# Delta-rule attention followed by an MLP: weight conversion and weight fetches redistributed over the engines, with a new order of all steps

## The chip, the cores and the metric

The kernel runs on one core of a Trainium2 chip. A core has a matrix engine (TensorE, "PE" in the profile; its weight loads are listed apart as "PEld"), a vector engine (VectorE, "DVE"), a scalar engine (ScalarE, "ACT"), a general engine (GpSimd, "POOL") and a sync engine (SyncE, "SP") that issues transfers. ACT and POOL issue transfers too. Each engine works through its own list of instructions in the order in which they were written. An instruction may wait for others on other engines; everything behind it on its own engine then waits as well. The metric is the time of the whole program on the device in microseconds (us).

## What is computed

```python
def _attn_ref(q, k, v, beta):            # 4 batches, 8 heads, 768 positions, 48 wide
    k_n = k / (norm(k) + 1e-06)
    state = zeros((B, H, D, D))
    for t in range(S):
        kt, vt, bt = k_n[:, :, t], v[:, :, t], beta[:, :, t, None]
        y[:, :, t] = einsum('bhd,bhde->bhe', q[:, :, t], state)
        v_old = einsum('bhde,bhd->bhe', state, kt)
        state = state + bt[..., None] * einsum('bhd,bhe->bhde', kt, vt - v_old)
    return y

def _moe_ref(x, g_ln, w_ch1, w_ch2):     # x: the heads side by side, 4 x 768 x 384
    xn = (x - mean) / sqrt(var + 1e-06) * g_ln
    return x + maximum(xn @ w_ch1, 0) @ w_ch2      # 384 -> 1536 -> 384
```

The two weight matrices arrive in 64-bit floating point; everything else, and the result, is 32-bit.

## The kernel before

**Stages.** The 768 positions are cut into twelve chunks (0 to 11) of 64, and the recurrence over the positions becomes, per chunk, products of small matrices with one triangular inverse. The names in the step list follow that. For chunk c, `G` is the product of the keys with themselves (`gram`), `P` that of keys and queries (`queries`), and `recur(c)` does the recurrence itself: `u` (the corrected values), `y` (the output), `s` (the state), then the layer norm of `y`, two transposes of it (L1199) and the copies into `xnt` (L1217), which is what the MLP of the chunk reads. `mlp(c)` multiplies `xnt` with the first matrix (L1424 for chunk 0), takes the maximum with 0 (L1432), and multiplies with the second (L1466 for chunk 0).

**The beginning.** For chunk 0 the inverse is made on PE by five rounds of doubling block sizes (`first_inverse`): in each round, for each of two groups of heads, a product E (L785), a masked copy on DVE (L790), a product Z (L803), transposes on DVE (L750) and three copies on ACT (L744). For later chunks the inverse is made row by row on DVE (`rows_inverse`, L925 and L932).

**The weights.** The 64-bit weights are read as pairs of 32-bit words and converted on the chip, in twelve pieces of 128 x 768 numbers (six of the first matrix, then six of the second). Piece i (counted from 0 in the code, so `i < 3` are the first three) is fetched by `fetch(i)` with two transfers of 384 KB each, and `convert(i)` turns it into 32-bit numbers by four steps: `hi`, the exponent trick on the high words (ACT, L599); a shift of the high words (DVE, L604); `lo`, the low words scaled by 2**-29 (ACT, L607); and the sum of both as integers (POOL, L617). The first three pieces are converted in a left and a right half of 384 columns each, the others whole. The fetched words lie in five buffers: the third, fourth and fifth piece in `words` 0 to 2, the first and second in the two halves of `h_all`. The sixth piece goes to the buffer of the third, the seventh to that of the fourth, the eighth to that of the fifth, so each of these fetches has to wait until the piece that lies there has been summed.

**The order.** All 3032 steps of the program are numbered in the order in which the code makes them (`Line.add`). The text `ORDER` (L156 on) lists the numbers in the order in which they are written out (`Line.emit`), and `in_this_order` keeps each engine to it. So each engine's sequence of instructions is fixed by this list: 954 steps on PE, 814 on DVE, 489 on ACT, 443 on POOL, 332 on SP. A letter `f` in the list stands for one idle matrix product. The numbers used below are: 224, 232, 212, 228, 220, 216 the `lo` steps of the first three pieces (first right, third right, first left, second right, third left, second left); 222 the `hi` step of the first piece's right half; 233 and 221 the sums of the third piece, right and left; 91 and 92 the fetches of the second piece; 235 and 234 those of the sixth, 355/356 of the seventh, 361/362 of the eighth; 246 and 244 `lo` and `hi` of the sixth; 307 and 305 the last two of four loads of the keys of chunk 2; 310 and 309 their transposes on PE (L635), 312 and 311 the copies of these on ACT (L640); 209 the scaling of the values of chunk 0 (POOL, L689); 653 and 655 two key loads that POOL issues; 329 and 331 `u` of chunk 0 (L1087), 333 and 334 its `y` (L1113), 353 its state (L1123); 313 and 325 the products G of chunks 2 and 3 (L850); 321/322 and 323/324 transposes of the keys of chunk 3 and their copies; 347 the first transpose of the layer norm (L1201) and 348 to 350 its copies (L1217); 567 and 569 the first two groups of the MLP (L1424).

Of the kernel before, what the change touches and what calls it, by code (L numbers as in the profile page):

```python
# [10 lines left out]
ALU = mybir.AluOpType  # L11
# [145 lines left out]
51-52 54 58 53 55 57 319 56 63 62 306 398 67 308 393 66 320 7 65 64 9 8 59 61 60 249 11 10 48 12 49 654 656 50 248 68 0 3 2 13  # L157
71-72 46 40 44-45 42-43 41 101-102 1 75 36 82-84 76-77 73-74 37 103 38 104 99 93 39 94 100 90 85-86 78 15 14 69 208 87 89 105-108
16-18 79-80 70 81 110 88 111 114-118 121 119 113 120 124 112 122 25 19-20 125 123 132 126 134 6 5 22 133 30 128 127 33 21 23 135
232 92 97 218 130-131 129 230 220 109 258 253 251 140 137 222 136 91 138 27 31 141 139 142 146 34 143 152 148 24 26 147 158 32 154  # L160
153 231 210 96 145 144 149-151 157 155-156 95 160 159 162 164 161 163 168 28-29 169-170 98 205 165 207 206 174 166 212 167 173 172
171 255 254 252 257 256 395 307 305 176 317 402 405 318 401 47 233 175 178 177 219 184 180 185-186 655 653 658 226 214 182-183 238
188 181 242 187 189 192 259 240 221 209 f 4 179 193 190 194 191 215 223 35 211 250 260-262 241 263 265 201 197 202 204 236 199 203
200 198 309 195 310 264 243 235 234 228 362 237 239 196 329-333 335 353 311 355 312 224 356 361 313-314 354 266-268 337 269-270
338 341 216 315 246 271-288 342-343 289-295 427 321-322 324 323 334 429 336 325-326 347 339-340 348-350 327 344 316 396 399 296
404 406 217 213 328 225 303 298 302 403 301 300 299 468 304 469 426 297 466-467 394 397 400 244 567 569 568 428 345-346 351 571
570 357 572 245 227 352 657 659 229 247 666 660 430 575 593 363 576 359 579-580 594 431 573 583 599 432 407 365 574 584 600 587
577-578 588 358 364 661 410 408 392 409 366 360 605 581 591 368 582 592 606 470 367 411 611 585-586 412 597 589-590 413 598 379
374 612 595-596 603 369 371 601 630 604 602 373 434 1068 668 465 471-474 476-482 414 483-485 667 415 370 372 670 1067 391 669 665
416 609 418 610 420 380 417 631-632 615-617 433 375 419 421-422 633-635 607 618 385 425 386 423-424 435-436 608 381 377 613  # L170
619-620 783 785 782 787 486-498 376 499-507 382 508-511 671-672 378 512 673 383 513 384 1080 916 786 789 788 779 784 918 614 437
440 442 445 441 387 438 443 439 636 621 637 662 638-639 514 444 446-447 450 389 663 674-675 515 388 516 390 1070 1072 677 517 448
790 451 518 449 452 519-539 622-623 457 640 453 641 624-626 1174 780 664 924 676 926 681 540 680 678-679 541 543 542 544 475 642
627 460 456 454 459 458 791 455 794 821-822 825 827 826 831-832 823 828 837 682 824 833 838 843 792 645-647 651 648-650 683-686
848 845 1082 781 1069 688 1071 1073 1084 846 1083 1074 847 1079 545 793 546 834 839 548 550 547 549 551 553 552 555 554 795
689-700 556 829 796 840 830 844 797 835 854 864 917 928 1173 927 925 930 929 923 931 1179 1181 849 922 463 701-705 800 802 798 855
805 706 806 799 1075 856-857 836 865 858 801 841 859 810 842 860 921 1180 643 1183 644 628 1184 629 1185 1365 1171 1178 1182
919-920 932 557 1086 852 862 850 464 851 861 853 866-868 811-812 871 817 1085 461-462 1542 1081 863 803 652 804 933 869 881 872
882 934 807 558 561 819 818 560 559 562 707-710 808-809 711 936 870 712-717 813 883-885 889 886 873-876 878-879 1544 877 887 1087
1554 880 814 816 815 566 564 563 820 565 935 937 972 896-901 890-894 938 973 1546 888 1556 1545 1555 1558 1541 1543 1091 1559  # L180
718-719 1186 978 939 941 720-725 1548 996 726-729 940 895 730 902 731-751 687 1076 979 943 1077 984 974-975 942 907-910 1088 1190
911-912 980 944 946-947 945 913 985 1089 951 981 948 990 976-977 986-987 991 982 1005-1007 983 988 1008-1010 989 994 992 1361 1368
1360 1370 1369 1078 1172 1372 1176 752 904 903 905 1090 997 906 756 753-755 1366 1177 952 949-950 953 955 969 954 1092 956 1093
1367 1371 757-758 1187 768 960 1175 1094 958 1373 1362 1095 957 1374 914-915 959 759 1011 964 999 1002 998 967 1000 968 1547 1003
1012 1022 993 1032 1023-1025 995 1015-1016 1033 1017 760 762 761 763 766 764 767 1188-1189 1549 1191 965-966 1013 1001 1004 1014
765 1018 1026-1027 1019 1034-1036 1020-1021 1192 1040-1041 1037 1042-1045 1375 1030 1557 970-971 1219 1223 1653 1655 1657 1659
1363 1652 1193 1196 769 1194 1842 1648 1654 1656 1658 1840 962 1096 963 1038-1039 1029 1238 1031 1028 1097-1098 1046 1099-1100
2030 1102 1234 1220-1221 773 772 1198 771 1058-1062 1239 1047-1048 1195 1201-1202 770 1197 1199-1200 1203-1204 1103 1560 1224 1376
774 776 775 1206 1049 1063 1050-1052 777 961 778 1227 1553 1377 1064 1207 1104 1053 1105 1205 1106-1110 1208 1111 1101 1112
1235-1236 1228-1229 1237 1230 1251 1231-1232 1252 1210 1233 1240-1241 1209 1253-1254 1378-1379 1246 1242 1247 1222 1243-1244 1270  # L190
1261 1055 1225 1262 1226 1380 1561 1245 2032 1054 1280 1248-1250 1258 1255-1256 1263-1264 1259 1257 1266-1267 1265 1113 1660 1114
1260 1271-1272 1268 1115-1116 1281-1282 1381 1647 1211 1650 1845 1056 1215 1364 1214 1847 1057 1839 1213 1846 1212 1646 1065 1848
1841 1838 1844 1066 2034 1275 1273 1117 1283 1118-1120 1274 1269 1284-1286 1382 1308 1276-1277 1309 1298-1299 1310 1383 1311 1292
1289-1291 1296 1287-1288 1312 1300 1313 1293 1295 1121-1123 1278 1124 1305 1301-1303 1325 1216 1304 1279 1306 1326 1315-1317
1217-1218 1294 1297 1307 1408 2035 1327 1318-1320 1328 1324 1322 2036 1323 1415 2042 1384 1125 1314 1333 1329-1330 1334-1338
1126-1132 1331 1340-1341 1409 1342-1345 1133-1135 1339 1419 2031 1332 1550 1410 1351 1423 1321 1412 1352 1413 1136-1138 1346 1411
1353-1355 1416 1356 1417 1385 1551 1562-1563 1418 2033 1427-1428 1139-1143 1414 1144-1145 1357 1146-1165 1429-1430 1424-1425 1420
1432-1433 1421 1387 1426 1439-1440 1661 1422 1431 1837 1552 1645 1849 1564 1166 1569 1851 1358 1568 1169-1170 1167-1168 1359
1436-1437 2043 1442 1347 1443-1445 1438 1386 1446-1448 1441 1449 1434 1450-1454 1461 1348 1456 1455 1435 1651 1850 1649 1349 2138
1457 1462-1465 1470 1350 1473 1489-1490 1458 1466 1479-1480 1467 1491 1481-1484 1492 1390 1662 1388-1389 1391 1468 1459 1674 1469  # L200
1663-1664 1676 1460 1485 1471 1476 1496 1486 1472 1497 1493-1494 1498 1506 1499 1567 1566 1477 1474 1487 1565 1475 1478 1504 1488
1668 1395 1392 1665 1667 1666 1669 1570 1670 1673 1671-1672 1396 1495 1397 1393 1399 1507 1514-1515 1500-1501 1508 1516 1675 1677
1517 1509-1510 1518 1503 1519 1511 1394 1398 1571-1572 1855 1852 1573-1574 1577 1512 1576 1513 2029 1578 1520 1579-1580 1502 1400
1403-1404 1402 1401 2044 1505 1678-1683 1686 1581-1582 1687 1583 1684 1532-1535 1521 1853 1856 1405-1406 1536 1522-1523 1843 1685
2037 1860 1407 1524 1704 1537 1705 1525-1526 1711 1706 1715 1708-1709 1723 1857 1859 1691 1688 1854 1689-1690 1584 1692 1585 1527
1586 1693 1538 1694 1587-1588 1866 1858 1861-1862 1707 1863 1695 1868 1710 1712-1713 2140-2141 2143 2145-2146 2133 1529 1719 1747
1716 1724 1717 1714 1720-1721 1589-1590 1757 1725-1726 1738-1739 2046-2047 2041 1865 1722 1718 1735 1732-1733 1727 1736 1740-1741
1734 1864 1742-1744 1728 1591-1594 1737 1595-1597 1745 1598 1729-1730 1599-1602 1748-1749 1758-1760 1750 1696 1698 1700 2144 2142
# [47 lines left out]
def kernel(  # L256
# [13 lines left out]
    nc = tc.nc  # L270
# [99 lines left out]
    add = line.add  # L370
# [185 lines left out]
    def tb_nat(i, kinds=(0, 1)):  # L556
# [1214 lines left out]
```

## Time and profile before

| | us |
|---|---|
| median of 3 runs | 513.96 |
| lowest and highest run | 513.07, 515.15 |
| the profiled execution | 513.69 |
| span of its trace | 512.0 |

The trace covers all but 1.69 us of the profiled execution. On one core the page's first part gives the busy time of each engine; the second cuts the span into 40 equal slices (12.8 us each), where a digit is the busy share in tenths and `PEclk` the granted clock of PE. The answers about single stretches give, for each engine, the busy time in us with the number of instructions, then the granted clock, the share of time in which the transfer engines were busy, and GB/s. The timeline gives start, length, engine, line, operation, output and input, shape and count, and in square brackets how long the engine had been idle before it and what ended that. An engine name with a q is its queue issuing a transfer.

### The profile page before, as it was taken

To read this page: it belongs to the slowest core of one execution; us is meant where nothing else is said; L and a number is where in the kernel's file an instruction comes from. 1 tells how busy PE (TensorE), PEld (TensorE's weight loads), DVE (VectorE), ACT (ScalarE), POOL (GpSimd) and SP (SyncE) were. 2 spreads that over 40 slices of the span, in tenths; PEclk is the share of its full clock that TensorE was granted. 3 is DMA by queue.
4 is the path that set the end of the run, shared out by engine and by line. 5 is a ranking of instruction groups with operands and counts; after the bars stand their busy time and mean duration, and the time that the engine had idled before them with its cause. 6 is when DMAs were issued, how large, how long until landed. Compare 5 with 4: busy or idle time off the path is not lost.

```text
span 512.0 us, 22780 instructions
## 1 busy us (share of the span) xinstructions
PE 481.8 (94%) x9968; PEld 446.6 (87%) x9968; DVE 357.4 (70%) x814; ACT 206.2 (40%) x462; POOL 282.3 (55%) x447
## 2 busy tenths in 40 slices
PE   4677799999999999999999999999999999999997
PEld 3566697768898899899988999999999999999996
DVE  4847658897988667999868898688788436253241
ACT  4577744633443144323334522524513425324130
POOL 8024385224874996784465574634462831654554
PEclk9777999999999999999999999999999999999999
DMA  9986787559456855364644563734424601212011
GB/s 128 257 188 124 211 150 179 123 148 159 82 92 127 204 103 81 85 120 113 136 96 70 105 132 102 130 86 103 88 39 98 140 8 46 52 46 50 2 32 31
DMA packets 181635, 54.56 MB, mean 107 GB/s; under 512 B 164888, under 2 KB 177312, under 8 KB 181536
## 3 DMA queue, kind: packets, MB, share of 16 engines
q1 hardware_dynamic: 168512, 40.10, 38.9%
q10 hardware_dynamic: 10816, 9.83, 6.5%
q0 software_dynamic: 2208, 3.17, 4.0%
q8 instruction: 78, 1.28, 1.1%
q14 instruction: 21, 0.17, 0.1%
HBM read 36.30 MB, written 16.78 MB: 104 GB/s over the span
## 4 chain that ended last, share of the span: by engine, by line
PE 83%; DVE 6%; DMA 3%; issue 3%; SPq 3%; ACT 2%; ACTq 0%; DVEq 0%
PE f L1541 29%; PE f L1325 21%; PE f L1444 6%; PE two L837 3%; PE f L1424 3%; SPq L409 3%; PE by L1051 2%; PE two L1051 2%; PE f L1466 2%; PE two L1106 2%; PE two L1123 2%; PE by L1113 2%; DMA kr<-in_k_dram 2%; PE f L803 1%; PE by L785 1%
## 5 line engine op out<-in xcount | busy, mean ns | idle before, releaser
L1528 POOL TENSOR_TENSOR h_all<-h_all 128x256 f32<-128x256 f32 x99 | 73.5, 755 | 20.4 <-DVE tmp L925 8.4
L1541 PE MATMUL f<-w_sb,h_all 128*128 128x192 f32 x396 | 79.2, 330 | 0.0
L1541 PE MATMUL f<-words,h_all 128*128 128x192 f32 x396 | 77.3, 330 | 0.0
L1348 DVE TENSOR_TENSOR h_all<-f,h_all 128x512 f32<-128x512 f32 x72 | 49.0, 686 | 28.5 <-PE f L1325 21.8
L1541 PEld LDWEIGHTS f<-w_sb,h_all 128*128 128x128 f32 x396 | 65.0, 190 | 1.5 <-issue 0.2
L1541 PEld LDWEIGHTS f<-words,h_all 128*128 128x128 f32 x396 | 64.8, 190 | 0.8
L1566 POOL TENSOR_TENSOR words<-h_all 128x128 f32<-128x128 f32 x66 | 30.0, 472 | 54.0 <-ACT h_all L1352 28.5
L1343 ACT COPY h_all<-f 128x512 f32<-128x512 f32 x45 | 26.2, 585 | 81.3 <-PE f L1325 52.3
L932 DVE TENSOR_TENSOR xb<-xb,tmp 128x31 f32<-128x31 f32 (+19 forms) x139 | 53.6, 386 | 3.5
L925 DVE TENSOR_TENSOR tmp<-xb,gb 128x31 f32<-128x31 f32 (+19 forms) x139 | 51.7, 372 | 4.1 <-POOL xb L912 0.3
L1352 ACT ACTIVATE h_all<-h_all 128x512 f32<-128x512 f32 x54 | 32.5, 626 | 32.5 <-DVE h_all L1348 32.4
L409 POOL DMA_DIRECT2D tb<-in_k_dram x64 | 41.9, 657 | 0.9 <-issue 0.7
L1325 PE MATMUL f<-xnt,w_sb 128*128 128x128 f32 x288 | 39.6, 278 | 0.1
L1325 PE MATMUL f<-x_new,w_sb 128*128 128x128 f32 x288 | 39.5, 277 | 0.0
L1325 PEld LDWEIGHTS f<-x_new,w_sb 128*128 128x128 f32 x288 | 36.4, 192 | 0.3
L1325 PEld LDWEIGHTS f<-xnt,w_sb 128*128 128x128 f32 x288 | 36.0, 192 | 0.6 <-DVE h_all L1348 0.2
L1444 PE MATMUL f<-xnt,w_sb 128*128 128x256 f32 x144 | 33.8, 385 | 0.0
L1559 DVE TENSOR_TENSOR o<-f,x 128x192 f32<-128x192 f32 x33 | 11.3, 348 | 28.4 <-PE f L1541 18.3
L1444 PEld LDWEIGHTS f<-xnt,w_sb 128*128 128x128 f32 x144 | 26.7, 190 | 3.8 <-DVE o L1475 0.4
L1541 PE MATMUL f<-w_sb,words 128*128 128x192 f32 x132 | 26.4, 330 | 0.3 <-DVE o L1559 0.3
L617 POOL TENSOR_TENSOR w_sb<-words 128x768 uint32<-128x768 uint32 (+1 forms) x11 | 14.9, 1365 | 16.4 <-ACT words L607 14.7
L1541 PEld LDWEIGHTS f<-w_sb,words 128*128 128x128 f32 x132 | 21.5, 190 | 0.9 <-DVE o L1559 0.6
(237 smaller groups left out, 976.1 us busy)
## 6 DMA issues: line engine op xcount, KB each, us to landing
words<-in_moe_w_ch_dram ACTq DMA_DIRECT2D x20, 384.0 KB, 4.9
gd<-gsb SPq DMA_DIRECT2D x11, 512.0 KB, 3.7
v<-in_v_dram SPq DMA_DIRECT2D x24, 192.0 KB, 4.1
kr<-in_k_dram SPq DMA_DIRECT2D x46, 96.0 KB, 3.5
out_dram<-o SPq DMA_DIRECT2D x46, 96.0 KB, 2.4
xld<-xlt SPq DMA_DIRECT2D x9, 384.0 KB, 2.3
xnt<-xld SPq DMA_DIRECT2D x36, 96.0 KB, 2.9
tb<-in_q_dram SPq DMA_DIRECT2D x40, 64.0 KB, 3.7
```

Of the source, the lines that this page charges most:

```text
L409: add(eng, cost, lambda: QUEUE[eng].dma_start(out=out_, in_=in_), r, w, bulk=n * ns / 16e3, np=n, **kw)
L925: lambda j=j, n=n, w=w, t=t: nc.vector.tensor_tensor(out=t, in0=xv[:, 0:n, j : j + 1].to_broadcast([128, n, w]), in1=gv[:, j : j + 1, j + ...
L932: "DVE", dve(n * w), lambda t=t, rest=rest: nc.vector.tensor_tensor(out=rest, in0=rest, in1=t, op=ALU.subtract),
L1051: nc.tensor.matmul(dst[half(e), hp, j], src[drows(hp), (e if n else key_half(c, hp, e)) * GP + j], s_all[drows(hp), e, j], start=(n == 0 o ...
L1325: nc.tensor.matmul(wide(p[:, f : f + 128]), w[:, f : f + 128], r, start=start and i == 0, stop=True, skip_group_check=True)
L1343: add("ACT", act(512), lambda: nc.scalar.copy(o, p), pk, ok)
L1348: add("DVE", dve(512), lambda: nc.vector.tensor_tensor(out=o, in0=x, in1=y, op=op), [*xk_, *yk], ok)
L1352: add("ACT", act(512), lambda: nc.scalar.activation(o, o, ACTF.Relu, scale=scale), [], ok)
L1444: nc.tensor.matmul(p[:, 0:TOK], w1_sb[:, t, f * 128 : (f + 1) * 128], xnt[:, t], start=(t == 0), stop=(t == KC - 1))
L1528: add(eng, cost, lambda: e.tensor_tensor(out=out_, in0=x, in1=y, op=op), r, w, port=2 if eng == "Pool" else 1, pr=-2)
L1541: lambda f=f, t=start and f == order[0]: nc.tensor.matmul(p[:, 0:D2], lhs(f), rhs[:, f], start=t, stop=(f == order[-1]), skip_group_check=True
L1566: lambda f=f + i: e.tensor_tensor(out=s3[f], in0=one(0, 0)[0](f), in1=one(1, 0)[0](f), op=ALU.subtract),
```

## The change

Three things are edited.

```diff
-    RUN = 128
+    RUN, LOWS = 128, 3
...
         for a in range(2):
             dma(
-                "ACT", dst[:, a], src[:, a].rearrange("p (b x) -> p b x", x=2 * RUN), 384, 54,
+                "SP" if 5 <= i < 8 else "ACT", dst[:, a], src[:, a].rearrange("p (b x) -> p b x", x=2 * RUN), 384, 54,
                 w=[("wd", BUF[i], a)], after=after, **kw,
             )
...
-        add("ACT", 0.17 + 1.15e-3 * n, lambda: nc.scalar.mul(lo, lo, 2.0**-29), wk, lk, **kw)
+        if i < LOWS:
+            add("Pool", 0.19 + 1.67e-3 * n, lambda: nc.gpsimd.tensor_scalar(out=lo, in0=lo, scalar1=2.0**-29, scalar2=None, op0=ALU.mult), wk, lk, **kw)
+        else:
+            add("ACT", 0.17 + 1.15e-3 * n, lambda: nc.scalar.mul(lo, lo, 2.0**-29), wk, lk, **kw)
```

The six `lo` steps of the first three pieces go to POOL, and six transfers of 384 KB are issued by SP instead of ACT. The numbers of the steps stay what they were. The whole text `ORDER` is replaced; nearly all of its lines differ, and of the 954 PE steps 780 stand at another place among PE's steps, by at most 19 places. It has one `f` before and after. Taken apart by engine, the part that matters for the first 60 us is this (numbers in the order of the lists; `...` where steps are left out):

```
PE    before  ... 192 f 190 194 201 197 309 195 310 329 331 333 353 313 427 321 322 334 325 347 426 567 569 351 ...
PE    after   ... f 192 190 194 197 201 195 310 329 331 309 333 334 313 321 322 353 347 325 427 426 569 567 351 ...
ACT   before  ... 235 234 228 362 335 311 355 312 224 356 361 314 354 341 216 315 246 324 323 429 336 326 348 349 350 ...
ACT   after   ... 226 312 311 335 246 314 315 341 336 244 323 324 354 348 349 350 326 327 344 ...
POOL  before  65 64 9 8 59 61 60 249 10 ... 47 233 655 653 658 221 209 250 264 243 239 217 213 225 ...
POOL  after   9 10 65 64 59 7 249 654 46 8 ... 47 42 43 656 224 232 212 49 228 233 220 209 653 655 221 50 250 264 225 243 239 216 248 658 213 229 217 ...
SP    before  ... 395 307 305 317 402 405 318 401 316 396 399 296 ...
SP    after   ... 318 395 235 397 307 305 401 234 317 402 405 361 396 394 362 400 399 355 406 316 356 296 ...
```

On ACT, 91 comes right behind 222 in the new list, and 92 some way ahead of it. In the old list ACT has the `lo` steps 232 and 220 and the fetch 91 ahead of or around 222.

More of the change, by code (lines that the diff above doesn't have):

```diff
@@ L161 @@
[L161 to L172, printed above, removed]
@@ L249 @@
[L249 to L251 removed]
+53 51 56 55 58 57 9-10 65 64 52 54 2 11-12 33 13 3 0 63 66 62 306 320 319 308 59 7 249 654 46 8 44 40-41 45 48 60-61 47 68 72 71
@@ L252 @@
+2941 2926 2956 2946 2949 2957-2958 2980 2897 2889 2898 2888 2950 2959 2951 2960 2970-2974 2981-2982 2975 2983-2985 2976 2987-2989
+2986 2964 2961-2962 2967 2963 2968 3005 2990 3006-3007 2977 2997 2965 2978 2966 2969 2979 2998 2991-2992 2999-3001 3008 3002
+3009-3010 3003 2995 3004 2994 3012-3017 2996 3011 2993 3018 3023-3028 3019-3020 3029 3021 3030 3022 3031
 """
```

175 lines of the change are left out of this document (92 added, 83 removed).

## The prediction

> **What bounds the kernel now.** I read the page first, then the busy time by stretches, the timeline of PE, and the chain of waits for the first 66 us.
>
> ```profile
> span 512.0 us, 22780 instructions
> PE 481.8 (94%) x9968; PEld 446.6 (87%) x9968; DVE 357.4 (70%) x814; ACT 206.2 (40%) x462; POOL 282.3 (55%) x447
> ```
> ```profile
> 13.00:26.00 13.00, 7.99 (x296) 7.07 (x292) 10.93 (x33) 7.77 (x19) 0.81 (x2) 0.76 1.01 259
> 26.00:39.00 13.00, 9.38 (x324) 8.15 (x324) 6.59 (x20) 9.30 (x26) 4.07 (x6) 0.76 0.84 185
> 39.00:52.00 13.00, 9.72 (x338) 8.18 (x339) 9.66 (x31) 9.53 (x21) 5.06 (x6) 0.82 0.60 122
> 52.00:65.00 13.00, 10.13 (x308) 8.87 (x300) 8.05 (x32) 10.62 (x23) 5.30 (x7) 1.00 0.71 209
> 65.00:78.00 13.00, 13.00 (x320) 12.51 (x319) 7.87 (x14) 5.52 (x19) 11.39 (x13) 1.00 0.81 149
> ...
> 200.00:300.00 100.00, 97.64 (x1968) 93.18 (x1967) 86.52 (x185) 38.06 (x80) 61.53 (x104) 1.00 0.49 101
> ```
>
> PE is busy 94% of the span. What it lacks lies in front: in the four stretches from 13 to 65 us it is busy 7.99, 9.38, 9.72 and 10.13 us of 13, from 65 on 13.00 of 13. Later the worst stretch, 200 to 300, lacks 2.36 us. So the time is the moment at which PE becomes dense plus a mass of products that the change doesn't touch. An earlier start of the MLP of chunk 0 is worth its full length, as long as nothing later runs dry; work saved on ACT or added on POOL is worth nothing by itself. The start is here:
>
> ```profile
> 18.07 0.69 PE L785 MATMUL by<-qt,gsb 64*64 64x64 f32 x32 [3.67 <-DVE qt L773]
> ...
> 20.18 1.99 PE L803 MATMUL f<-xt,gsb 64*64 64x64 f32 x64 [0.82 <-DVE gsb L790]
> ...
> 43.68 1.15 PE L803 MATMUL f<-xt,pt 64*64 64x64 f32 x64
> 44.90 0.66 PE L635 MATMUL f<-ident,kr 128*128 128x128 f32 x4
> ...
> 46.91 0.65 PE L635 MATMUL f<-ident,kr 128*128 128x128 f32 x4
> ...
> 60.53 1.58 PE L1424 MATMUL f<-xnt,w_sb 128*128 128x128 f32 x12
> ```
> ```profile
> 50.79 0.84 issue
> ...
> 56.75 1.10 issue
> ```
>
> The last products Z of the inverse begin at 43.68; the key transposes 309 and 310 at 44.90 and 46.91; the MLP (567 and 569) at 60.53. From 310 to the MLP it is 13.6 us, with 0.84 and 1.10 us of it waits that the profile explains by nothing ("issue").
>
> **Part one: the six `lo` steps.** Each is an ACT instruction of 0.57 us:
>
> ```profile
> L607 ACT ACTIVATE h_all<-h_all 128x384 uint32<-128x384 uint32 x4 | 2.3, 568 | 0.0
> ...
> L1528 POOL TENSOR_TENSOR h_all<-h_all 128x256 f32<-128x256 f32 x99 | 73.5, 755 | 20.4 <-DVE tmp L925 8.4
> ```
> ```profile
> 33.64 0.61 POOL L490 COPY pt<-u 128x512 f32<-128x512 f32 x1 [19.83 <-DVE x L477]
> 34.22 0.82 POOL L617 TENSOR_TENSOR w_sb<-words 128x384 uint32<-128x384 uint32 x1
> 35.00 1.94 POOL L409 DMA_DIRECT2D tb<-in_k_dram  x3
> ...
> 39.00 1.47 POOL L689 TENSOR_TENSOR v<-v,knat 128x768 f32<-128x768 f32 x1
> ...
> 46.41 0.44 POOL L912 COPY xb<-db_b 128x16 f32<-128x16 f32 x1 [1.35 <-DVE gb L915]
> ```
>
> ACT loses 6 x 0.57 = 3.4 us. On POOL no row shows this operation. A copy with one input takes 0.61 us for 512 columns, so 0.46 by proportion for 384; a float operation with two inputs takes 755 ns for 256, so 1.13 for 384; the integer sum of the same 384 columns takes 0.82. I take 0.82, as the shape and type are the same, and keep 0.46 to 1.13. Three of the six (224, 232, 212) come where POOL sits idle for 19.83 us, until 33.64, and cost nothing there; were that idle time gone, they would cost 2.5 us. One, 216, comes behind 264, with the sums that the MLP's first group needs at 57 us. The other two, 228 and 220, come ahead of 209 and 221, and this is a new chain, worked out next.
>
> **Part two: the fetches on SP, and what they hold up.** The fetch 235 goes out only when 221 has summed the third piece. Behind it on SP now stand 397, then 307 and 305, the keys of chunk 2, which 310 and 309 on PE read, and behind these on PE stand 329 and the rest of chunk 0. Before, SP asked for these keys at 32.64, 12 us ahead of their use:
>
> ```profile
> 26.10 0.56 ACT L599 ACTIVATE h_all<-h_all 128x384 f32<-128x384 f32 x1
> ```
> ```profile
> 32.64 2.07 SPq L409 DMA_DIRECT2D kr<-in_k_dram  x2
> ...
> 58.40 0.63 SPq L409 DMA_DIRECT2D v<-in_v_dram  x1
> ```
> ```profile
> kr<-in_k_dram SPq DMA_DIRECT2D x46, 96.0 KB, 3.5
> ```
> ```profile
> DMA to landing us min/median/max: 3.4/4.9/7.6
> ```
> ```profile
> DMA to landing us min/median/max: 8.5/8.5/8.5
> ```
>
> (The last two are the transfers of weight words into `words` and into `h_all`.) In order: 222 runs at 26.10 before; its words are asked for a little later and ACT is a little freer, so I leave it. It ends at 26.7; the fetch 91 behind it takes 0.5 (an issue of SP takes 0.63), 27.2; the words land 4.9 later (the median into `words`; bounds 3.4 and 8.5), 32.1. POOL waits for them with 228: 0.82; 233: 0.82; 220: 0.82; 209: 1.47; 653 and 655: 2/3 of 1.94 = 1.29; 221: 0.82; together 6.0, so 38.1. SP then issues 235, 397, 307, 305: 4 x 0.63 = 2.5, 40.6. The keys took 3.5 by themselves, but now follow 384 KB of weights in SP's queue; I take the 4.9 of those (bounds 3.5 and 7.6): 45.5. **310 can start at 45.5, against 46.91.** Were the keys no bound, it could start when Z of the last round has ended, 43.68 + 1.15 = 44.8, less what the rounds themselves gain. They can gain at the very start:
>
> ```profile
> 6.31 0.23 DVE L442 TENSOR_TENSOR u<-u 128x64 int32<-128x64 int32 x1 [3.13 <-POOL u L436]
> ```
>
> DVE waits 3.13 us for an index pattern that POOL makes late; the new list has it as POOL's second instruction. Only part of that reaches the end of the rounds, since the keys of chunk 0 land later than this; I take 1 us of the possible 0 to 3.1, so 43.8 for the floor.
>
> The rule of the Trainium skill that bears on this is in "DMA: Bandwidth & Descriptors", section "Queues, rings and completion order": an engine takes the queue rows that have work in turn, but what stands in one row in order. By it the pieces would hurt more in SP's row, in front of the keys, than in ACT's, beside them. The bound 7.6 would then be the nearer one, the start of 310 at 48.2, and the whole time about 513.3. No row here shows a small load behind a piece in one queue.
>
> **Part three: from 310 to the MLP.** What ACT carries in that time sets it, as its instructions follow back to back:
>
> ```profile
> 45.31 0.91 ACTq L409 DMA_DIRECT2D words<-in_moe_w_ch_dram  x2
> ...
> 49.82 0.48 ACT L1151 COPY x<-two 128x384 f32<-128x384 f32 x1 [1.72 <-PE two L1113]
> ...
> 50.20 0.59 ACT L640 COPY kt<-f 128x512 f32<-128x512 f32 x1
> ...
> 51.15 0.57 ACT L607 ACTIVATE h_all<-h_all 128x384 uint32<-128x384 uint32 x1
> 51.15 0.63 ACTq L409 DMA_DIRECT2D words<-in_moe_w_ch_dram  x1
> 53.64 0.58 ACT L858 COPY gsb<-f 128x512 f32<-128x512 f32 x1 [1.92 <-PE f L837]
> 54.12 0.81 ACT L1135 COPY s_all<-two 128x768 f32<-128x768 f32 x1
> 54.81 0.31 ACT L1163 ACTIVATE rstd<-mv,eps 128x1 f32<-128x1 f32 x1
> ...
> 55.92 0.93 ACT L607 ACTIVATE words<-words 128x768 uint32<-128x768 uint32 x1
> ...
> 60.01 0.89 ACT L1217 ACTIVATE xnt<-by,g_sb 128x128 f32<-128x128 f32 x3
> ```
>
> Before, three `lo` steps (228, 224, 216: 1.7 us) and six issues (the first two 0.91, the last 0.63) lay in this stretch, and the state, the second `y` and the transposes stood in another order. After: 310, 329, 331 and 309 on PE take 2.5 us (0.65 for each set of transposes, 0.6 for each half of `u`). From then on ACT has 311 0.59, 335 0.48, 246 0.93, two copies 314 and 315 at 0.58, 341 0.31, 336 0.48, 244 0.93, two copies 323 and 324 at 0.59, 354 0.81, 348 to 350 0.89: 7.75 us. Behind 354 PE still has two sets of transposes (427, 426: 1.3 us), ending about when the copies do plus 0.5. So the MLP starts 2.5 + 7.75 + 0.5 = 10.7 us after 310, if nothing stalls; with the two waits of before (1.9 us) 12.7. I take the middle, 11.7: 45.5 + 11.7 = 57.2, against 60.53.
>
> **The sum.** -3.3 us at the start of the MLP. The six transfers that left ACT cost SP 6 x 0.63 = 3.8 us; beyond the keys they lie ahead of 316 and 296, which wait for copies and for DVE anyway, so 0 (a microsecond each for those if not). POOL's extra steps may slow DVE while both run: 0.2 us, a guess between 0 and the 2.5 of part one. The rest of the program, where 780 of 954 products change places, I put at 0, with -2.4 (the gap between 200 and 300) and +3 as ends. So -3.1: from the profiled execution's 513.69 (span 512.0 plus 1.69) to **510.6**. The median shown is 0.27 higher, within the spread of the three runs.
>
> **The rivals.**
>
> *More is won.* The keys arrive in time (30.6 for the second piece, 3.5 for the keys put 310 at its floor, 43.8) and no wait of the "issue" kind falls into the stretch: the MLP at 54.5, 6.0 earlier, 507.7. For it speaks that both waits have no cause in the profile; against it that each took the better end of its range. A full clock would help further: the granted clock is 0.76 and 0.82 from 13 to 52, and 64 products took 1.99 us there against 1.15 later. Of 27 us of PE work in these stretches a clock of 1.00 would take off at most 0.24 x 17.4 + 0.18 x 9.7 = 5.9. The 3.67 us for which PE waits ahead of 18.07 stay for the most part, so I expect the same two slow stretches. The Trainium skill, "TensorE: Matmul & The Clock Gate", Part 1, has the clock fall to half after a window of some 3.4 us without enough work; fewer gaps could so pay twice.
>
> *Given back later.* The MLP starts 3 us earlier, but its followers don't: DVE, 86.5 us busy of the 100 from 200 on, makes the row inverses, and PE waits for it at one of the chunks. 2.5 of the 3.1 come back: 513.1. For it speaks that PE was already dry by 2.36 us there; against it that the first row inverse (264 on POOL) starts at about 39 us, soon after 221, instead of 46.41, so DVE's chain moves up as well.
>
> *Slower: the new chain through POOL and SP.* Mechanism and place: 228 waits for the second piece at POOL's head, 221 behind it, 235 and the keys behind that on SP, 310 on PE. At the upper ends, 8.5 for the piece and 7.6 for the keys, 310 starts at 45.5 + 3.6 + 2.7 = 51.8, the MLP at 63.5, 3.0 us later than before: 516.7, and more if POOL takes longer for a `lo` than any row says. It decides against the change from a start of 310 at 60.53 - 11.7 = 48.8 on, 3.3 us behind my estimate. For it speaks that 8.5 was measured into the very buffer; against it that four pieces were under way then, and fewer here.
>
> *The edit does less than it says*: ACT's issues ran beside its operations (the one at 51.15 while ACT computed), so taking them off frees less than their length. This is in the sum, which counts only operations.
>
> **How the numbers follow.** A change of 0.5% is about what a measurement of this kernel can tell from none; that is 511.4 and 516.5. Forecast (-3.1; its own range 508.8 to 512.2) 0.50, of which 0.08 stays within 0.5%; more won 0.12; given back 0.14, mostly within, 0.03 slower; the chain through SP 0.24, 0.03 of it within. Faster 0.42 + 0.12 = 0.54; same 0.08 + 0.11 + 0.03 = 0.22; slower 0.03 + 0.21 = 0.24. The range goes from 506.5, a little beyond "more won", to 517.5, a little beyond the slower case.
>
> **What would show it.** In the changed kernel's timeline: six POOL steps of 0.46 to 1.13 us on 128x384 words, three of them before the second piece lands; SP idle ahead of the first `words` transfer until POOL's sum 221; the wait of the key transposes named "DMA kr"; the MLP's first group at 57 (54.5 to 60); ACT without gaps ahead of it; from 65 on PE busy as before. I am wrong if the first group starts after 60.5, or if it starts near 57 and the stretches behind it lack as much PE time as the front gained.

## The result, and the profile after

| kernel | chip | median us | runs | ratio to the kernel before, 95% interval | mean granted clock of the runs |
|---|---|---|---|---|---|
| before | first | 512.95 | 18 | 1 | |
| changed | first | 509.76 | 18 | 0.9937 [0.9919, 0.9955] | 0.989 |
| before | fourth | 512.63 | 22 | 1 | 0.982 |
| changed, measured again | fourth | 510.97 | 12 | 0.9982 [0.9955, 1.0009] | 0.987 |

In the first measurement the changed kernel is faster by 0.6%. In the second, on another chip, it is faster by 0.2%, and that interval includes 1, so this measurement alone does not tell the change from none. The forecast was 510.6 us. The profiled execution of the first measurement took 510.69 us, 1.69 more than its span.

The page of the changed kernel, span and busy time:

```profile
span 509.0 us, 22783 instructions
...
PE 480.2 (94%) x9968; PEld 445.5 (88%) x9968; DVE 362.7 (71%) x814; ACT 204.5 (40%) x456; POOL 289.8 (57%) x453
```

The stretches of the changed kernel that were shown of the one before:

```profile
13.00:26.00 13.00, 8.55 (x284) 7.26 (x272) 9.11 (x29) 8.12 (x21) 4.39 (x5) 0.74 0.97 264
26.00:39.00 13.00, 9.98 (x324) 8.63 (x324) 7.17 (x24) 8.99 (x25) 8.62 (x10) 0.74 0.70 164
39.00:52.00 13.00, 9.46 (x405) 8.11 (x400) 12.10 (x37) 9.99 (x21) 7.88 (x9) 1.00 0.73 165
52.00:65.00 13.00, 11.73 (x242) 10.89 (x237) 7.72 (x22) 10.01 (x25) 6.98 (x9) 1.00 0.93 219
65.00:78.00 13.00, 12.16 (x377) 11.07 (x369) 8.25 (x22) 5.12 (x16) 6.29 (x9) 1.00 0.80 186
91.00:104.00 13.00, 11.18 (x279) 7.29 (x278) 11.80 (x19) 5.87 (x10) 10.67 (x12) 1.00 0.69 151
...
200.00:300.00 100.00, 98.73 (x1978) 94.46 (x1981) 87.16 (x186) 36.62 (x74) 63.00 (x104) 1.00 0.52 109
```

The stretch from 91 to 104 in the kernel before:

```profile
91.00:104.00 13.00, 13.00 (x356) 9.14 (x358) 10.57 (x24) 8.24 (x15) 4.89 (x4) 1.00 0.61 131
```

The reader is to see two things. From 52 to 65 PE is busy 11.73 us instead of 10.13: the MLP has begun earlier. And a new hole has opened from 91 to 104 (11.18 of 13, where it was 13.00), where DVE is busy 11.80 and POOL 10.67. From 65 to 78 PE is busy 12.16 instead of 13.00, so part of the gain is given back there already. The timeline of PE in the changed kernel says where:

```profile
16.16 0.69 PE L789 MATMUL two<-qt,gsb 64*64 64x64 f32 x32 [2.90 <-DVE qt L777]
...
43.62 0.66 PE L639 MATMUL f<-ident,kr 128*128 128x128 f32 x4 [0.44 <-ACT xt L748]
...
55.27 0.39 PE L1428 MATMUL f<-xnt,w_sb 128*128 128x128 f32 x2
56.35 1.38 PE L1428 MATMUL f<-xnt,w_sb 128*128 128x128 f32 x10 [0.70 <-POOL w_sb L621]
...
103.21 0.55 PE L1205 MATMUL by<-ident,xln 128*128 128x128 f32 x3 [1.82 <-DVE xln L1173]
```

The first E is 1.9 us earlier than before, the key transposes 310 are 3.3 us earlier (46.91 before), the MLP 5.3, or 4.2 if one counts from 56.35, where it runs on. In the trace of the second measurement (N below) these are 1.2, 2.4 and 3.5 us (E at 16.85, 310 at 44.54, the MLP at 57.06). At 103.21, ahead of the transposes of chunk 1's layer norm, PE waits 1.82 us for DVE. The chain on POOL and SP that the prediction worked out, in the changed kernel:

```profile
26.03 1.24 POOL L609 TENSOR_SCALAR h_all<-h_all 128x384 uint32<-128x384 uint32 x1
...
28.01 1.21 POOL L609 TENSOR_SCALAR h_all<-h_all 128x384 uint32<-128x384 uint32 x1 [0.46 <-DVE words L605]
29.29 0.83 POOL L621 TENSOR_TENSOR w_sb<-words 128x384 uint32<-128x384 uint32 x1
...
34.29 0.85 POOL L621 TENSOR_TENSOR w_sb<-words 128x384 uint32<-128x384 uint32 x1
```
```profile
35.30 1.68 SPq L410 DMA_DIRECT2D words<-in_moe_w_ch_dram  x1
...
37.65 1.31 SPq L410 DMA_DIRECT2D kr<-in_k_dram  x2
```

In one execution each of the kernels F, K and M below PE ran far slower (690.28, 958.45 and 689.52 us); these are left out of the ratios, and as the profiled execution of F and K was such a one, no times of PE are taken from those two traces.

### The profile page after: what moved, and what is told of

Same layout as the page of the kernel before. It is cut to its first block, busy times and chain, and to the rows that moved or that the text cites. A ratio compares the mean times of both kernels' runs of the same rounds, so it can differ in the third digit from the quotient of the medians.

```text
span 509.0 us, 22783 instructions
## 1 busy us (share of the span) xinstructions
PE 480.2 (94%) x9968; PEld 445.5 (88%) x9968; DVE 362.7 (71%) x814; ACT 204.5 (40%) x456; POOL 289.8 (57%) x453
## 3 DMA queue, kind: packets, MB, share of 16 engines
q8 instruction: 78, 1.28, 1.1%
## 4 chain that ended last, share of the span: by engine, by line
PE 80%; DVE 9%; issue 3%; DMA 2%; ACT 2%; SPq 2%; POOL 2%; DVEq 0%
PE f L1545 28%; PE f L1329 23%; PE f L1448 6%; DVE xb L936 3%; PE two L841 3%; PE by L1055 2%; PE f L1470 2%; PE two L1055 2%; PE by L1117 2%; PE two L1110 2%; SPq L410 2%; DVE tmp L929 2%; PE f L1428 2%; PE two L1127 1%; PE by L1009 1%
## 5 line engine op out<-in xcount | busy, mean ns | idle before, releaser
L936 DVE TENSOR_TENSOR xb<-xb,tmp 128x31 f32<-128x31 f32 (+19 forms) x139 | 59.8, 430 | 3.8
L1312 POOL TENSOR_TENSOR x_new<-xnt 128x128 f32<-128x128 f32 x27 | 13.0, 486 | 23.2 <-PE f L1329 10.6
```

Of the source, the lines that this page charges most:

```text
L936: "DVE", dve(n * w), lambda t=t, rest=rest: nc.vector.tensor_tensor(out=rest, in0=rest, in1=t, op=ALU.subtract),
```

## The experiments

Each kernel was compared with the kernel before on the same chip: A to D on one, F, G, H and J on a second, K, L, M and the changed kernel again (N) on a third, the "fourth" of the table above. The two columns in the middle are from one trace each, in us.

| kernel | first MLP product | first MLP product of chunk 1 | median us, all runs | ratio, 95% interval | mean granted clock of the runs |
|---|---|---|---|---|---|
| before | 60.53 | 112.91 | 513.40, 513.49, 512.63 | 1 | 0.982 on each of the three chips |
| changed | 55.27 | 110.01 | 509.76 | 0.9937 [0.9919, 0.9955] | 0.989 |
| changed again (N) | 57.06 | 110.61 | 510.97 | 0.9982 [0.9955, 1.0009] | 0.987 |
| A | 59.36 | 114.22 | 512.30 | 0.9980 [0.9953, 1.0007] | 0.984 |
| B | 54.70 | 108.53 | 510.49 | 0.9963 [0.9939, 0.9988] | 0.989 |
| C | 55.76 | 111.14 | 511.50 | 0.9971 [0.9951, 0.9991] | 0.987 |
| D | 61.31 | 113.47 | 513.25 | 1.0014 [0.9985, 1.0043] | 0.981 |
| F | | | 511.63 | 0.9954 [0.9926, 0.9982] | 0.988 |
| G | 57.40 | 111.06 | 510.57 | 0.9942 [0.9918, 0.9965] | 0.986 |
| H | 57.62 | 111.58 | 513.46 | 1.0003 [0.9972, 1.0035] | 0.983 |
| J | 58.87 | 110.50 | 510.66 | 0.9948 [0.9920, 0.9976] | 0.989 |
| K | | | 518.60 | 1.0102 [1.0061, 1.0143] | 0.979 |
| L | 55.57 | 107.77 | 508.43 | 0.9904 [0.9873, 0.9936] | 0.990 |
| M | 55.96 | 107.15 | 509.00 | 0.9914 [0.9882, 0.9947] | 0.989 |

Two rows of one and the same kernel (changed, N) lie 1.8 us apart at the first MLP product. N's inverse starts 0.7 us later, and its PE stands 1.28 us more, at 53.97, for what the profile calls "issue". So a single trace shows mechanisms well and sizes under 2 us badly. The clock adds to this: PE's granted clock falls to 0.50 for some us at a time, and not at the same places in each trace. It is 0.50 from 34 to 43 us in the kernel before and from 31 to 37 in the changed one, and even from 48 to 58 in A and from 51 to 57 in J, where it makes the first MLP product late.

### Which part of the change does it: A, B, C, D

A keeps the new order alone; B adds the fetches on SP to it, C the `lo` steps on POOL; D has both edits in the old order.

```diff
 A and B
-    RUN, LOWS = 128, 3
+    RUN, LOWS = 128, 0
 A and C
-                "SP" if 5 <= i < 8 else "ACT", dst[:, a], ...
+                "ACT", dst[:, a], ...
 D
 ORDER = """
-53 51 56 55 58 57 9-10 65 64 52 54 2 11-12 33 13 3 0 63 66 62 306 ...
+51-52 54 58 53 55 57 319 56 63 62 306 398 67 308 393 66 320 7 65 64 ...
```

> The new order, with all lo steps and all fetches on ACT again, at their places in the list. Theory 1 (the MLP of chunk 0 starts earlier because ACT is relieved between 43 and 57 us): ACT gets back three lo steps among the rounds and one (216) plus six issues around 310, and the two fetches of the eighth piece stand ahead of the key copies and wait for POOL's sum of the fifth piece (43.6 to 45 us in the changed kernel); first MLP product at 57 to 58 instead of 55.3, ratio to the kernel before 0.997 (0.995 to 1.000). Theory 2 (the order does it alone, the two moves are incidental): first product at 55 to 56, ratio 0.994.

> The new order and the three fetches on SP, but the six lo steps on ACT (0.57 us each instead of 1.24 on POOL). Theory 1: ACT has 1.7 us more among the rounds and 0.57 around 310, POOL's chain to the sum 221 has 2 to 3 us less; first MLP product at 56 to 57, ratio 0.995 to 0.998. If POOL's chain to 221, SP's fetch and the keys were the bound, this kernel would be faster than the changed one: first product before 55, ratio 0.992.

> The new order and the six lo steps on POOL, but all fetches on ACT. Theory 1: the eighth piece's fetches hold the key copies on ACT until the sum of the fifth piece, about 45 us; first MLP product 1 to 2 us later (56.5 to 57.5), ratio 0.996 to 0.998. If the queue of SP behind the fetches (keys, gram, row inverse) was what cost time, this kernel is faster: ratio 0.992 or less.

> The old order of all steps with both moves. Theory 1 by ACT's load alone: from u of chunk 0 to the MLP ACT carries 1.7 us of lo steps and six issues less, so the first MLP product at 58.5 to 59.5 instead of 60.5, ratio 0.996 to 0.998. Theory 2 (order alone): ratio 1.000; slower than before if the longer lo steps on POOL (1.24 us) hold up the row inverse of chunk 1 or the sums: 1.002.

A, fetches on ACT; the timeline of PE around 310, then that of ACT:

```profile
42.74 0.63 PE L639 MATMUL f<-ident,kr 128*128 128x128 f32 x4 [1.07 <-DMA words<-in_moe_w_ch_dram]
...
48.88 0.77 PE L1117 MATMUL by<-u,pt 64*64 64x48 f32 x17 [3.01 <-issue]
```
```profile
43.75 2.29 ACTq L410 DMA_DIRECT2D words<-in_moe_w_ch_dram  x2
...
46.98 1.05 ACT L644 COPY kt<-f 128x512 f32<-128x512 f32 x2
```

And B, fetches on SP, the timeline of ACT:

```profile
43.90 0.59 ACT L644 COPY kt<-f 128x512 f32<-128x512 f32 x1 [0.36 <-PE f L639]
```

The wait ahead of 310 is longer with the fetches on ACT (1.07 us in A and 1.61 in C, put down to a transfer of `words`, against 0.44 in B, put down to ACT), but 310 does not start later for it: at 42.74 and 43.70, against 43.24 in B and 43.62 in the changed kernel. What the fetches hold is ACT's next work. In A they go out at 43.75, when the first of two sums on POOL has ended, and the copies 312 and 311 of the transposed keys follow at 46.98 (47.06 in C); in B the first of them runs at 43.90. So the fetches did hold ACT's copies, by some 3 us, and moving them removes that. How much of it reaches the MLP is not shown: C has its first product at 55.76 all the same, and A's 59.36 contains the 3.01 us of "issue" and the stretch at half the clock. B reaches the first MLP product at 54.70 with all `lo` steps still on ACT: in this one trace the `lo` steps were not needed on POOL for an early start. None of the four came out in the range that its first theory gave for this product (57 to 58, 56 to 57, 56.5 to 57.5, 58.5 to 59.5). B's is the value that was to speak for POOL's chain as the bound, but its ratio is not the 0.992 that belonged to it. By time the four cannot be ranked: A, B and C lie between 0.996 and 0.998, and the full change, measured on two other chips at 0.9937 and 0.9982, lies on both sides of them. What stands apart is D: in the old order both edits together gain nothing, and its interval lies above that of the first measurement of the whole. D was expected at 0.996 to 0.998. Its trace, POOL and then PE:

```profile
59.65 2.39 POOL L623 TENSOR_TENSOR w_sb<-h_all 128x384 uint32<-128x384 uint32 x3 [5.39 <-DVE xb L938]
```
```profile
61.31 1.60 PE L1430 MATMUL f<-xnt,w_sb 128*128 128x128 f32 x12 [1.49 <-POOL w_sb L623]
```

In the old order the last three sums of the first pieces stand on POOL behind the row inverse of chunk 1 on DVE, and the MLP waits for them. The edits need an order made for them. Whether the order alone (A, whose interval just includes 1) gives less than the whole is not shown.

### What brought the beginning forward: G and K

G writes the two index patterns 9 and 10 behind five other POOL steps. K gives POOL's first 21 steps the order of before, but behind them three `lo` steps stand ahead of the copies 43 and 41, and 221 with its fetches 235 and 234, as well as 361 and 362, stands later. So K changes more than the copies.

```diff
 POOL, changed kernel and G
-9 10 65 64 59 7 249 654 46 8 ...
+65 64 59 7 249 9 10 654 46 8 ...
 POOL, changed kernel and K
-9 10 65 64 59 7 249 654 46 8 44 40 41 45 48 60 61 47 42 43 656 ...
+7 65 64 9 8 59 61 60 249 10 48 49 654 656 50 248 46 40 44 45 42 224 232 212 43 41 228 220 47 ...
```

> The changed kernel with the two index patterns as sixth and seventh instruction of POOL instead of first and second. Theory 1 (they are what brought the inverse of chunk 0 forward): the first E goes from 16.2 back to about 18 us, the key transposes 310 and the MLP come 1 to 2 us later, the ratio is 0.996 to 0.998. Rival (the keys of chunk 0 and ACT set the start): the first E stays at 16 to 16.7, the ratio stays at 0.993 to 0.995.

> The changed kernel with POOL's first 24 steps in the order of the kernel before: loads and a large fill first, the eight copies of 512 columns from about 10 us on. Theory 1 (these copies, standing beside DVE's chain of short steps for the first keys, stretch it; moved ahead of it they brought the first E forward): the short DVE steps between 9 and 14 us take 0.4 to 0.7 us instead of 0.15 to 0.2, the first E goes from 16.2 to 17.5 to 18.5, the MLP starts 1 to 2 us later, the ratio is 0.996 to 0.999. Rival (the order on DVE, ACT and PE did it): the first E stays below 16.8, the ratio stays at 0.993 to 0.995.

The first E of G, in the timeline of PE:

```profile
16.06 0.69 PE L792 MATMUL two<-qt,gsb 64*64 64x64 f32 x32 [2.75 <-DVE qt L780]
```

The theory of G falls: E stays at 16.06, and the ratio at 0.9942. In G DVE takes up the second pattern at 5.05 us (1.44 in the changed kernel, 6.31 in the kernel before), and still waits for the keys behind it. The wait of 3.13 us for a late index pattern, which the prediction credited with 1 us, was covered by the wait for the keys. In its place the timelines of the kernel before, DVE and then POOL, offer this:

```profile
9.86 0.61 DVE L665 TENSOR_TENSOR ndb<-knrm 128x8 f32<-128x8 f32 x1
...
13.25 0.57 DVE L665 TENSOR_TENSOR ndb<-knrm 128x8 f32<-128x8 f32 x1
```
```profile
9.85 0.61 POOL L490 COPY pt<-u 128x512 f32<-128x512 f32 x1
...
10.98 2.28 POOL L490 COPY xt<-u 128x512 f32<-128x512 f32 x4
```

The same step in the changed kernel, where POOL's copies have begun at 5.43 us, while DVE waits for keys:

```profile
9.02 0.17 DVE L669 TENSOR_TENSOR ndb<-knrm 128x8 f32<-128x8 f32 x1
```

0.57 and 0.61 us beside POOL's copies, 0.17 without them, for eight numbers a row. K was to show that these copies set the first E. The first half of its theory holds: beside the copies the step takes 0.57 and 0.45 us on DVE again. The rest cannot be read: K is 1.0% slower than the kernel before, far beyond what was expected of it, and the moved copies got a wait that had not been counted. K's timelines of POOL and DVE:

```profile
22.88 1.28 POOL L494 COPY xt<-u 128x512 f32<-128x512 f32 x2 [11.01 <-DVE xb L469]
```
```profile
29.83 0.42 DVE L797 COPY_PREDICATED gsb<-x,by 128x256 f32<-128x256 int32 x1 [6.15 <-POOL gsb L494]
```

POOL stands 11.01 us ahead of the copies; three `lo` steps follow, and only then the copy into `gsb` for which DVE, in the middle of the inverse, waits 6.15 us. So K shows that POOL's first steps can cost more than the whole change brings, and leaves open how much of the 1.9 us comes from the copies beside DVE. That reading stands on the rows of the kernels and was not shown by an experiment of its own. A rival was not tested: the second group of transposes of chunk 0's keys (PE, L635 and L639) starts at 9.91 in the kernel before and at 8.86 in the changed one, both times after a wait put down to the keys' transfer, so earlier keys may be a part of it.

### How much room the new chain has: H

```diff
-lambda: nc.gpsimd.tensor_scalar(out=lo, in0=lo, scalar1=2.0**-29, ...)
+lambda: [nc.gpsimd.tensor_scalar(out=lo, in0=lo, scalar1=x, ...)
+         for x in ([2.0**-29, 1.0, 1.0, 1.0] if (i, c0) == (2, 0) else [2.0**-29])]
```

> The changed kernel with the lo step 220 done four times (three of them multiply by 1), so that POOL's sum 221, and with it the fetch 235 and the keys 307 and 305 on SP, come 3.7 us later. Theory 1 (the chain through POOL and SP has 1.7 us of room at the most): 310 starts 2 to 3.7 us later, at 45.6 to 47.3, its wait is put down to the keys, and the ratio is 0.998 to 1.001. Rival (310 waits for the inverse on PE and ACT alone, with more room): 310 stays within 0.5 of 43.6, and the ratio at 0.993 to 0.995.

H, timelines of POOL, SP and PE:

```profile
30.64 5.18 POOL L610 TENSOR_SCALAR words<-words 128x384 uint32<-128x384 uint32 x4
```
```profile
40.79 1.30 SPq L410 DMA_DIRECT2D kr<-in_k_dram  x2
```
```profile
45.22 1.09 PE L642 MATMUL f<-ident,kr 128*128 128x128 f32 x4 [1.85 <-ACT h_all L600]
```

The keys are asked for 3.1 us later than in the changed kernel (40.79 against 37.65). The wait of 310 is put down to ACT, but ACT's last copy of the inverse ends at 44.00 here, and 310 starts at 45.22; in the changed kernel it starts 0.05 us behind that copy. The second of the two transfers was asked for at 41.5 and landed 3.5 us later, at 45.0. So the keys held 310 by about 1.2 us, an inference from these rows, and the chain had about 1.9 us of room; against the changed kernel's 43.62 the shift is 1.6 us and the room 1.5, against N (keys asked for at 38.22, 310 at 44.54) 0.7 and 1.9. Theory 1 gave 1.7 us of room at the most, which fits, and a shift of 2 to 3.7, which is more than any of these. The ratio is 1.0003, against 0.9942 for G on the same chip: 3.9 us more of POOL's work (5.18 against 1.23) cost all that the change had brought. Where it cost this is not shown, as H's first MLP product is only 0.2 us later than G's, and its span 0.3 us longer (510.2 against 509.9). So the hold that the slower rival of the prediction names is real; that it alone makes the loss is not shown.

### Where the rest went: F, J, L, M, N

F closes up the layer norm of chunk 1: both copies of `y` together on ACT, both halves' DVE steps together. J is F with the sums 229 and 217 written out 41 places earlier in the list (the expectation says 16). L is F with POOL's sum 390, its loads 1068, 1067, 1080, 1070, 1082, 1081, 1072 and its fills 677, 392, 391 written out behind the layer norm. M is J with that. N is the changed kernel.

In J and M, POOL's own sequence stays that of F and L. What moves is a wait that the code adds (`emit`, "shared port"): a POOL step that is not a load waits for the last DVE step marked `port` that stands ahead of it in the list. In J the two sums so wait for the layer norm of chunk 0, no longer for the whole row inverse. In L, 390 moves ahead of three loads and waits for the second `xln` of chunk 1, and the rest of POOL stands behind it.

```diff
 ACT, changed kernel and F
-441 383 389 442 614 447 663 450 675
+441 442 383 389 614 447 450 663 675
 DVE, changed kernel and F
-439 443 444 445 515 446 516 448 449 517 790 451 452 518
+439 443 444 445 446 448 449 451 452 515 516 517 790 518
 ORDER, F and L
-384 ... 1068 1067 1080 390 1070 677 1082 392 1081 1072 391 444 ... 451 452 515
+384 ... 444 ... 451 452 390 1068 1067 1080 1070 677 1082 392 1081 1072 391 515
 ORDER, F and J
-342-343 287-295 ... 229 217
+342-343 229 217 287-295 ...
```

> The changed kernel with one thing moved: in chunk 1 the two copies of y stand together on ACT (the two lo steps of the last pieces behind them), and the layer norm's steps stand together on DVE, ahead of three row steps and a transposition of queries. Theory 1 (what the front gained is given back ahead of chunk 1's layer norm): the wait of 1.82 us ahead of its transposes goes below 0.5, the MLP of chunk 1 starts at about 108.5 us instead of 110.0, and the ratio to the kernel before falls from 0.9937 to 0.990 to 0.991. Rival (the products behind are limited elsewhere and take the time back again): the wait goes, but the ratio stays at 0.993 to 0.995.

> The first of these kernels (chunk 1's layer norm close together) and also two sums of the second piece (229 and 217) written out 16 places earlier, right behind the first layer norm of chunk 0, so that POOL need not wait for the whole row inverse of chunk 1. Theory 1 (POOL's sums are what holds the first MLP products): the 0.70 us ahead of the MLP's third product goes, its bulk starts at about 55.6, and the ratio is 0.988 to 0.990. Rival (the sums then hold DVE, and with it the second layer norm): the start does not move by more than 0.3 us, and the ratio is that of the first kernel.

> The kernel F (chunk 1's layer norm close together) and POOL's last weight sum, its seven key loads and its three fills written out behind that layer norm, so that they wait for it. Theory 1 (DVE is the bound from 91 to 113 us, and POOL's work beside it takes some 3 us from it; F alone only moved the wait from the transposes to the residual sum o): both xln steps take 0.5 us, there is neither the wait for xln nor the one for o, PE is busy in all but 0.5 us of 98 to 117, and the ratio is 0.989 to 0.992. Rival (POOL's work then falls on the row steps behind and costs DVE the same there): PE waits 1 to 2 us for o, ratio 0.993 to 0.996.

> The kernel L with the two sums 229 and 217 written out earlier as in J. Theory 1: the waits for w_sb, xln and o are all gone, ratio 0.987 to 0.991. Rival (as in L; and the sums hold DVE in the front): ratio that of L or above it.

> The changed kernel itself, on the chip of the three others, to compare them with: 0.992 to 0.9955, its runs at a mean granted clock of about 0.989 against 0.982 for the kernel before. If the granted clock were no part of the gain, the mean over the runs would be the same for both kernels.

F gains nothing over G, on the same chip the nearest to the change (0.9954 against 0.9942). J, which shares its edit and whose trace can be read, says why; PE, then DVE, then POOL:

```profile
103.76 0.49 PE L1208 MATMUL by<-ident,xln 128*128 128x128 f32 x3
...
113.80 1.56 PE L1451 MATMUL f<-xnt,w_sb 128*128 128x256 f32 x6 [1.85 <-DVE o L1482]
```
```profile
99.09 0.48 DVE L1176 TENSOR_SCALAR xln<-x,mv,rstd 128x384 f32<-128x384 f32 x1
...
99.68 2.41 DVE L1176 TENSOR_SCALAR xln<-x,mv,rstd 128x384 f32<-128x384 f32 x1
...
113.24 0.51 DVE L1482 TENSOR_TENSOR o<-f,x 128x384 f32<-128x384 f32 x1
```
```profile
99.14 1.97 POOL L413 DMA_DIRECT2D tb<-in_k_dram  x3
101.12 2.28 POOL L624 TENSOR_TENSOR w_sb<-words 128x768 uint32<-128x768 uint32 x1
```

The wait of 1.82 us for `xln` is gone, and by 113.80 PE has waited 1.85 us, put down to `o`, the residual sum that reads the results of chunk 0's MLP out of `f`. In between DVE is nearly full, in J from 98 to 104 and from 104 to 111:

```profile
98.00:104.00 6.00, 6.00 (x142) 3.93 (x141) 5.82 (x10) 2.95 (x6) 5.99 (x7) 1.00 0.65 166
104.00:111.00 7.00, 7.00 (x149) 4.98 (x148) 6.52 (x17) 1.82 (x7) 4.68 (x7) 1.00 0.47 117
```

So moving its steps about only moves the wait. What could be saved is in the durations: one `xln` takes 0.48 us alone and 2.41 beside POOL's loads and sum (in the kernel before the two took 1.18 and 1.24). L takes POOL's work away from there. L, timeline of DVE; then the stretch from 98 to 117 of L, and of N:

```profile
96.35 0.48 DVE L1176 TENSOR_SCALAR xln<-x,mv,rstd 128x384 f32<-128x384 f32 x1
...
96.94 0.48 DVE L1176 TENSOR_SCALAR xln<-x,mv,rstd 128x384 f32<-128x384 f32 x1
...
108.45 0.51 DVE L1482 TENSOR_TENSOR o<-f,x 128x384 f32<-128x384 f32 x1
```
```profile
98.00:117.00 19.00, 19.00 (x259) 14.62 (x259) 18.14 (x42) 6.00 (x15) 8.35 (x12) 1.00 0.78 165
```
```profile
98.00:117.00 19.00, 17.15 (x285) 12.72 (x275) 18.20 (x39) 5.42 (x14) 7.70 (x10) 1.00 0.66 149
```

PE is busy all 19 us in L, 17.15 in N. On the same chip L has 0.9904 [0.9873, 0.9936], N 0.9982 [0.9955, 1.0009]; the intervals do not meet. Not all of that is shown to come from here: of the 2.84 us by which L's MLP of chunk 1 is earlier than N's, 1.49 stand already at the first MLP product, ahead of the steps that L moves. L is the fastest kernel of this study, with a median of 508.43 against 510.97 for the change and 512.63 before. Theory 1 holds for L. For the early sums nothing is shown: J's first MLP product is at 58.87, but behind a wait of 1.78 us of "issue" and the stretch at half the clock; and M is no faster than L, which has no wait for `w_sb` at the first products without them. N came out above the 0.992 to 0.9955 expected of it.

## Why the prediction was right, point by point

**The start of the inverse.** I took 1 us of 0 to 3.1 for an earlier index pattern. The first E came 1.9 us earlier (N: 1.2), but G shows that the index pattern has no part in it. The size was within the range by luck, as the reason was wrong.

**The second piece.** I let its fetch go out when 222 had ended, at 27.2, and its words land at 32.1. That step failed twice. In the changed kernel 222 runs at 24.04, 2.06 earlier than before, and the transfer's own row stands ahead of it, not behind it:

```profile
23.33 0.37 ACTq L410 DMA_DIRECT2D h_all<-in_moe_w_ch_dram  x1
...
24.04 0.56 ACT L600 ACTIVATE h_all<-h_all 128x384 f32<-128x384 f32 x1
```

An issue on an engine's queue need not wait for the operation written before it (N: 23.86 ahead of 25.46), although the opening of this document lets everything behind a step wait with it. So 228 at 28.01 found its words there and waited 0.46 us for DVE.

**The price of a `lo` on POOL.** 0.82 was taken, 0.46 to 1.13 were the bounds; it took 1.21 to 1.24 us. The copy and the integer sum of the same columns were both too cheap as models. The two steps ahead of 221 cost 0.8 us more than planned, which the early second piece paid for.

**The keys.** SP's issues: 1.68 us for the fetch 235, not 0.63; but 221 started at 34.29, not 37.3, and the keys were asked for by 38.96, not 40.6. 310 started at 43.62 (forecast 45.5), near the floor of 43.8 that the inverse sets. The term was mis-sized by 1.9 us because the chain was thought to bind, and it did not. The price taken for keys behind a piece in SP's queue, 4.9 with bounds of 3.5 and 7.6, was a fair one: they landed after 5.4 us in B and 3.5 in H.

**From 310 to the MLP.** 11.7 was forecast; 11.65 it was (N: 12.52), and 12.7 to the product at which the MLP runs on. The middle between no stall and the stalls of before was a fair choice: 1.12 us of "issue" and 0.70 for `w_sb` remained, in N 0.94 and 1.28 of "issue".

**The sum.** -3.3 at the MLP was forecast, -5.3 (N: -3.5) came. "The rest at 0" failed: PE lost 1.82 us at chunk 1's layer norm, so the rival "given back later" holds in part, at chunk 1, and not at the chunks from 200 us on, where PE is busier than before (98.73 against 97.64). The rows of J and L show what it was: DVE slowed by POOL. That POOL's work slows DVE was in the sum as 0.2, but for the `lo` steps; the price fell due at the sums and loads of 95 to 103 us. The front won more and the rest lost more than the sum had it, and the two errors cancelled: that 509.76 came so close to 510.6 was luck. In N the front came out at its size, the rest still lost its 1.85 us at the layer norm, and 1.7 us in all remained.

**The clock.** I expected the slow stretches to stay. Up to 39 us they did (0.74 in place of 0.76), from 39 to 52 the clock rose from 0.82 to 1.00. In the runs the mean granted clock rose from 0.982 to 0.989 and 0.987 (that of the kernel before is on record for the three later chips, not for the first). Within the runs of the kernel before, a straight line through time against clock falls by 125, 204 and 262 us for a full unit on the three chips. With 200, the 0.007 is worth some 1.4 us of the 3.2, and 0.005 some 1.0 of the 1.7. This is a correlation: fewer holes in PE's work raise the clock and shorten the time as well. The Trainium skill, "TensorE: Matmul & The Clock Gate", Part 1, has the clock fall after a window of some 3.4 us without enough work; the table agrees loosely, in that the kernels with the latest first MLP product (before, D) have the lowest clock of those with a usable trace, and no run here sets the clock by itself.

**The slower rival** had its place right, but the chain ran 3 us ahead of the sum (221 ended at 35.1, not 38.1). H shows that it begins to hold 310 when it stands some 1.5 to 1.9 us later than in the changed kernel, not from where on it decides the time.

## What to carry to other kernels

When work moves to an engine that shares something with a busy one, price not only the moved steps but what stands beside them later: look for steps of one form whose duration differs by a factor, and see what the other engine does at those moments. A wait that disappears when steps are reordered, and comes back a few microseconds later under another name, points to a full engine behind it; here only faster work on that engine helped. Before pricing a transfer, read the queue's own rows, as they may stand ahead of the operation that is written before them.

## What the runs showed of the hardware

- **POOL, one input against two.** Scaling 128x384 words of 32 bits (every second word) took 1.21 to 1.24 us on POOL, the sum of 384 columns from two operands 0.82 to 0.85, and the scaling on ACT 0.57. One input was not cheaper than two.
- **DVE beside POOL.** `xln`, 128x384, takes 0.48 us in L, where POOL is kept away from it. In the changed kernel it stands beside POOL's sum at 98.14 and its fill at 101.97, timelines of DVE and POOL:

```profile
98.52 1.97 DVE L1173 TENSOR_SCALAR xln<-x,mv,rstd 128x384 f32<-128x384 f32 x1
...
102.03 1.13 DVE L1173 TENSOR_SCALAR xln<-x,mv,rstd 128x384 f32<-128x384 f32 x1
```
```profile
98.14 1.58 POOL L621 TENSOR_TENSOR w_sb<-words 128x768 uint32<-128x768 uint32 x1
...
101.97 0.97 POOL L1682 MEMSET xt<- 128x1024 f32 x1
```

The second one ends at 103.16, the fill at 102.94. The Trainium skill, "SBUF — State Buffer", section "SBUF: two separate sides", has DVE and GpSimd share one pair of ports under an exclusive lock: for certain operations of DVE (in a mode with two ports, or with two inputs from SBUF against a GpSimd operation that reads SBUF) the later one waits for the whole instruction of the earlier. Whether `xln` is of that kind no row shows. The first `xln` agrees roughly: the sum ends at 99.72, 0.48 more makes 100.20, and it ends at 100.49. The second agrees less: 0.48 behind the fill makes 103.42, and it ends 0.26 us ahead of that.

- **An issue of 384 KB on SP** took between 0.55 and 2.14 us in the changed kernel (the one shown 1.68), while loads of keys took 0.65 each.
- **The same kernel on two chips**, in two measurements, came out at 0.9937 [0.9919, 0.9955] and 0.9982 [0.9955, 1.0009] against the kernel before.
